# Reordering the last three heads of each attention round in a two-layer decode kernel

## The chip, the cores and the metric

The kernel runs on one core of a Trainium2 chip. The metric is device time in microseconds (us) of one launch; smaller is better. Everything is 32-bit floating point. The core's engines are TensorE (PE in the profile; its weight loads are PEld), VectorE (DVE), ScalarE (ACT), GpSimd (POOL, used only in the first microseconds) and SyncE (SP), which issues nearly all loads from device memory.

## The reference

A decode step for 4 sequences with one token each, model width 640. An attention layer and a dense layer, and then both again with the same weights:

```python
x = x + A(layernorm(x))     # 32 heads of 128, keys and values: the last 1024 of 4096 positions
x = x + B(layernorm(x))     # relu(x @ w1) @ w2, inner width 1728
x = x + A(layernorm(x))
x = x + B(layernorm(x))

# A, for each head h
q = x @ wq[:, h]                          # 4 x 128
p = softmax(q . k[b, h] * 128 ** -0.5)    # 4 x 1024, each sequence has its own cache
o = p . v[b, h]                           # 4 x 128
out += o @ wo[h]                          # back to 640
```

Each head needs its part of wq, its keys and values for four sequences, and its part of wo; one pass over all heads and both dense matrices is some 160 MB, read twice apart from what is kept on chip between the rounds.

## The kernel before, in words

**Records and buffers.** The host lays each head's data out as one record of 128 partitions by 9472 columns: wq (640 columns, from WQ), keys (4096, from K), values (4096, from V), wo (640, from WO). On chip there are five record buffers, `slot0` to `slot4`, used in turn, and a sixth, `ring`, which holds one more head of round 0 (head 26, SIXTH) and later the dense matrices w1 and w2 in pieces. The heads 27 to 31 stay in the five slots at the end of round 0 and are the first five of round 1, so they are not loaded again.

**Loads.** The list `items` holds all loads in an order written out by hand. `pump` issues from its head, on SP's queue, as long as the next piece's place on chip is free in the program's order; `done(key, lo, hi)` marks columns as used and pumps again. A load then waits on SP, at run time, for the instructions that last read its place. At most eight loads are under way, since a completion semaphore is used again only when its last load has landed. Most records are one load. The last three heads of a round, called a, b and c here, come in pieces in the order that `ending` gives. In round 0 the wo parts of the last five heads follow, and then w1 and w2, in eleven pieces, through three places of `ring`; each waits for the products on an earlier piece. In round 1 w1 goes into `ring` as a whole and w2 into a slot that came free.

**One head.** All engines run strictly in the program's order (`InOrder`). For a head:

- `query`: five products give q (128 x 4) in the first columns of a PSUM buffer `sc_ps[s]`, and DVE copies it to `qT`.
- `scores`: eight products give the scores of four sequences in the two banks of `sc_ps[s]`.
- `softmax`: DVE takes the maximum and scales it, ACT takes the exponential in place, with its sum in `tot[s]`.
- `weights`: DVE makes 1/sum (into `spread`, `rtot`, `mrt`), and for each half transposes the scores into `t_ps` and multiplies them into `wT`.
- `values`: four products for each half, with `wT` as the stationary operand, into `o_ps` (or, for the last head of a round, into the second bank of `sc_ps[0]`).
- `picks`: DVE picks the four wanted blocks out of that, in four operations, into `on`.
- `output_T`: a product with `pick` transposes it, DVE copies it to `oTs[:, i]`.
- `project`: four products with wo add it to the accumulator `acc`.

In the trace a 32-bit product stands as two passes, so `project` shows x8 and `query` x10.

**The loop of a round.** In steady state, while head n's values are taken, head n+1's scores and head n+2's query are interleaved: scores(n+1), softmax, values(n), picks, query(n+2), output_T, project, weights(n+1). Before the change it runs for all but two heads; the last two follow by hand, the second half of the weights of b behind the softmax of c. The outputs of the last `late` heads of a round (5 in round 0, where their wo comes last; 2 in round 1) are kept in `oTs`, and those in round 0 are projected at the end.

**Between attention and dense layer.** `center` sums `acc` over its columns, takes off the mean and prepares the squares; `mlp` takes the products with w1, in five blocks, with `deviation` (a product, DVE, a square root on ACT) behind the first, then relu on ACT, two transposes on DVE and the products with w2 in pieces. `busy(n)` is a product of n columns whose result nobody reads; it only keeps TensorE at work.

Of the kernel before, what the change touches and what calls it, by code (L numbers as in the profile page):

```python
# [32 lines left out]
F32 = mybir.dt.float32  # L33
AF = mybir.ActivationFunctionType
OP = mybir.AluOpType
# [3 lines left out]
P = 128  # L39
# [4 lines left out]
EPS = 1e-5  # L44
# [50 lines left out]
def decode_kernel(ctx: ExitStack, tc: tile.TileContext, xf, rec, w1, w2, out):  # L95
# [3 lines left out]
    ps = ctx.enter_context(tc.tile_pool(name="ps", bufs=1, space=PSUM))  # L99

    xT = sb.tile([P, FD], F32, name="xT")
    scratch = sb.tile([P, 480], F32, name="scratch")
    wT = scratch[:, :128].rearrange("p (i c j) -> p i c j", i=2, c=16)
    on = [scratch[:, 128:256], scratch[:, 288:416]]
    x_sb = scratch[:, :FD]
    same = scratch[:, FD:FD + P]
    blocks = xT.rearrange("p (k j) -> p k j", j=32)[:, :, :B]
    spread = scratch[:, 256:288]
    hT = scratch.rearrange("p (m j) -> p m j", j=32)
    oTs = sb.tile([P, LATE, B], F32, name="oTs")  # L110
    qT = sb.tile([P, B], F32, name="qT")
    of_batch = sb.tile([P, B], F32, name="of_batch")
    of_block = sb.tile([P, 4], F32, name="of_block")
    pick = sb.tile([P, B], F32, name="pick")
    mrt = sb.tile([P, B], F32, name="mrt")
    small = sb.tile([P, 14], F32, name="small")
    nmax, rtot, rstd, eps, eps_dh, ones, unused, sums, tot0, tot1 = (small[:, i:i + 1] for i in range(10))
    squares = small[:, 10:]
    tot = [tot0, tot1]
    slot = [sb.tile([P, REC], F32, name=f"slot{i}") for i in range(NS)]  # L120
    ring = sb.tile([P, RING], F32, name="ring")
# [23 lines left out]

    dve.tensor_reduce(of_block, same[:, :16].rearrange("p (c j) -> p c j", j=4), op=OP.add, axis=AX.X)
    dve.tensor_reduce(pick, same[:, :32].rearrange("p (c j) -> p j c", j=4), op=OP.add, axis=AX.X)
    dve.memset(small, EPS)
    dve.memset(eps_dh, EPS * DH)
    dve.memset(ones, 1.0)  # L150
    dve.memset(o_ps, 0.0)
# [24 lines left out]
    def ending(r, hs, late):  # L176
        a, b, c = hs[-3:]
        end = WO if late else REC
        for h, lo, hi in ((a, 0, V), (b, 0, V), (a, V, end), (c, 0, V), (b, V, end), (c, V, V + VH), (c, V + VH, end)):
            piece(r, h, lo, hi)  # L180
        if late:
            for h in hs[-1:] + hs[-LATE:-1]:
                piece(r, h, WO, REC)
# [116 lines left out]
    def xblock(k):  # L300
        return xT[:, 32 * k:32 * k + B]

    def query(r, h, s):
        q = sc_ps[s][:, :B]
        key = ("rec", r, h)
        for k in range(KB):
            pe.matmul(q, cols(key, WQ + k * DH, DH), xblock(k), start=(k == 0), stop=(k == KB - 1))
        done(key, WQ, K)
        dve.tensor_copy(qT, q)

    def scores(r, h, s, first=False):
        key = ("rec", r, h)
        for i in range(2):
            for b in range(B):
                pe.matmul(sc_ps[s][32 * b:32 * b + 4, 512 * i:512 * i + 512], qT[:, b:b + 1].to_broadcast([P, 4]),
                          cols(key, K + 512 * (B * i + b), 512), start=True, stop=True)
            done(key, K + VH * i, K + VH * i + VH)
            if first and i == 0:
                deviation(of_batch, eps_dh, float(DH))
                act.activation(unused, eps, AF.Exp)  # L320

    def softmax(s, first=False):

# [3 lines left out]
        dve.tensor_tensor(nmax, nmax, rstd, op=OP.mult)  # L327
        act.activation(sc_ps[s], sc_ps[s], AF.Exp, bias=nmax, scale=rstd, accum_out=tot[s])

    def weights(s, parts=(0, 1)):  # L330
        if 0 in parts:

            dve.transpose(spread, tot[s].to_broadcast([P, 32]))
            dve.reciprocal(rtot, spread[:, 0:1])
            dve.tensor_scalar(mrt, of_batch, rtot, None, op0=OP.mult)
        for i in parts:
            dve.transpose(t_ps, sc_ps[s][:, 512 * i:512 * i + 512])
            dve.tensor_tensor(wT[:, i], t_ps.rearrange("p (c j) -> p c j", j=32)[:, :, :B],
                              mrt.unsqueeze(1).to_broadcast([P, 16, B]), op=OP.mult)

    def values(r, h, last=False, fill=(0, 0)):
        key = ("rec", r, h)
        for i in range(2):
            for g in range(4):
                pe.matmul(outs[last][32 * g:32 * g + 16, :], wT[:, i, 4 * g:4 * g + 4, :].rearrange("p c j -> p (c j)"),
                          cols(key, V + VH * i + 512 * g, 512), start=(i == 0), stop=(i == 1))
            done(key, V + VH * i, V + VH * i + VH)
            for _ in range(fill[i]):
                busy(512, sc_ps[0])

    def picks(last):
        o, on_ = outs[last], on[last]
        dve.tensor_scalar(on_, o[:, :DH], of_block[:, 0:1], None, op0=OP.mult)
        for c in range(1, 4):
            dve.scalar_tensor_tensor(on_, o[:, DH * c:DH * c + DH], of_block[:, c:c + 1], on_, op0=OP.mult, op1=OP.add)

    def output_T(i, last=False):
        pe.matmul(outs[last][:, :B], on[last], pick, start=True, stop=True)
        dve.tensor_copy(oTs[:, i], outs[last][:, :B])

    def project(r, h, i, end):
        key = ("rec", r, h)
        for n in range(NB):
            pe.matmul(acc[32 * n:32 * n + B, :FD], oTs[:, i], cols(key, WO + n * FD, FD),
                      start=False, stop=end, skip_group_check=True)
        done(key, WO, REC)

    def mlp(r):


        h_ps, front, back = sc_ps[0][:, :512], t_ps[:, :224], sc_ps[0][:, 512:768]
        dve.memset(back[:, 208:240], 0.0)
# [16 lines left out]
        dve.transpose(scratch[:, 224:], back)  # L389
        key = ("w2", r)  # L390
        sizes = W2_SLOT if r else [size for name, size, _ in MLP_RING if name == "w2"]
        first = 0
        for i, size in enumerate(sizes):
            for s in range(first, first + size):
                m, n = TILES[s]
                w = cols(key, s * FD, FD)
                for part, q in ((m, n),) if m < 13 else ((13, n), (14, n + 2)):
                    pe.matmul(acc[32 * q:32 * q + B, :FD], hT[:, part, :B], w,
                              start=False, stop=(s >= len(TILES) - NB), skip_group_check=True)
            if r == 0 and i < len(sizes) - 2:  # L400
                busy(512)
            done(key, first * FD, (first + size) * FD)
            first += size
# [3 lines left out]
    pe.matmul(acc[:, :FD], ident, x_sb, start=True, stop=False, skip_group_check=True)  # L407
    for r in range(2):
        hs = order[r]
        late = LATE if r == 0 else 2  # L410
        center(r > 0)
        query(r, hs[0], 0)
        scores(r, hs[0], 0, True)
        softmax(0, True)
        query(r, hs[1], 1)
        weights(0)
        for n, h in enumerate(hs[:-2]):
            i = n - (H - late)
# [9 lines left out]
            weights(s, (0, 1) if n < H - 3 else (0,))  # L428
            if r == 0 and h == SIXTH:
                put_by()  # L430
            if r == 1 and hs[n + 2] == SIXTH:
                put_back()
        scores(r, hs[-1], 1)
        softmax(1)
        weights(0, (1,))
        values(r, hs[-2], 0, (0, 1))
        weights(1)
        picks(0)
        values(r, hs[-1], 1, (1, 0))
        picks(1)  # L440
        output_T(late - 2)
        for i in range(late - 3):
            project(r, hs[H - late + i], i, False)
        if late == 2:
            project(r, hs[-2], 0, False)
        output_T(late - 1, True)
        for i in (late - 3, late - 1, late - 2) if late > 2 else (1,):
            project(r, hs[H - late + i], i, i == late - 2 or late == 2)
        center(True)
        mlp(r)  # L450
    dve.tensor_copy(x_sb, acc[:, :FD])
# [39 lines left out]
```

## Time and profile before

| | |
|---|---|
| median of 3 runs | 719.93 us (717.66 to 720.21) |
| the profiled execution | 718.78 us, of which the span is 717.1 us |
| PE busy, share of the span | 516.8 us, 72% |
| DVE busy | 359.1 us, 50% |
| ACT busy | 93.0 us, 13% |
| read from memory | 301.56 MB, 421 GB/s over the span |
| mean granted TensorE clock | 0.797 of full speed |

Times in the rows are microseconds from the span's start. A timeline's row gives the start, the time taken, the engine, a line, the operation, out<-in with shapes, the number of instructions merged, and in brackets the idle time before and what ended it. A window's row gives the busy time of each engine (with the number of instructions that began), then the granted clock, the mean busy share of the 16 DMA engines, and GB/s. Nearly all instructions have line 87, the helper that keeps them in order, so groups are told apart by their tiles. Round 0's attention ends at about 367, its dense layer at about 391; round 1 follows to the end.

### The profile page before, as it was taken

How to read it: one execution, taken by the hardware profiler on the slowest of the kernel's cores; microseconds unless marked ns; L12 is line 12 of the kernel's file. 1: busy time of each engine (PE TensorE's matmuls, PEld its weight loads, DVE VectorE, ACT ScalarE, POOL GpSimd, SP SyncE). 2: the span in 40 equal slices, each digit the busy share in tenths (PEclk: the TensorE clock that was granted, in tenths of full speed). 3: DMA queues.
4: the chain of work that ended last, by engine and by line, in shares of the span. 5: the costliest groups of instructions: out<-in, count | busy, mean ns of one | idle time of the engine just before them, and what ended most of it. 6: DMA issues, size and time to landing. Idle time of an engine off the chain costs nothing.

```text
span 717.1 us, 8939 instructions
## 1 busy us (share of the span) xinstructions
PE 516.8 (72%) x3686; PEld 208.9 (29%) x3686; DVE 359.1 (50%) x1013; ACT 93.0 (13%) x145; POOL 1.1 (0%) x9
## 2 busy tenths in 40 slices
PE   4467756667686676857877998876857777666977
PEld 2132222313233232322223433332322322323323
DVE  3344545354455444545731677744545445444661
ACT  1201011010101101111200312201011010101111
POOL 0000000000000000000000000000000000000000
PEclk9977888687767777787899899977787578867797
DMA  9999999999999999999989999999999999999996
GB/s 377 435 435 434 435 428 430 436 434 433 430 430 434 435 432 435 431 427 424 424 345 333 409 434 428 444 425 434 436 433 436 422 431 436 438 434 418 429 426 286
DMA packets 15336, 302.21 MB, mean 421 GB/s; under 512 B 1712, under 2 KB 2240, under 8 KB 5312
## 3 DMA queue, kind: packets, MB, share of 16 engines
q1 hardware_dynamic: 15264, 301.64, 98.6%
q8 instruction: 29, 0.48, 0.2%
q14 instruction: 11, 0.09, 0.0%
q10 hardware_dynamic: 32, 0.01, 0.0%
HBM read 301.56 MB, written 0.08 MB: 421 GB/s over the span
## 4 chain that ended last, share of the span: by engine, by line
DMA 80%; PE 15%; DVE 3%; issue 1%; another core or an unknown queue 0%; DVEq 0%; SPq 0%
DMA slot<-rec 68%; PE sc_ps L87 8%; DMA ring<-rec 6%; PE o_ps L87 4%; DMA slot<-w 3%; PE acc L87 3%; DMA ring<-w 3%; DVE scratch L87 2%; DVE oTs L87 1%; DVE small L87 0%; DVE t_ps L87 0%; DVE ring L87 0%; DVE mrt L87 0%; DVE xT L87 0%
## 5 line engine op out<-in xcount | busy, mean ns | idle before, releaser
L87 PE MATMUL sc_ps<-xT,slot 128*128 128x4 f32 x620 | 99.5, 287 | 148.9 <-DMA slot<-rec 146.6
L87 PE MATMUL sc_ps<-slot,qT 128*4 128x512 f32 x992 | 197.1, 935 | 1.0 <-DVE qT L87 1.0
L87 PEld LDWEIGHTS sc_ps<-xT,slot 128*128 128x128 f32 x620 | 95.4, 238 | 203.7 <-issue 194.0
L87 ACT ACTIVATE sc_ps<-sc_ps,small 128x1024 f32<-128x1024 f32 (+1 forms) x68 | 76.6, 1127 | 551.4 <-DVE small L87 551.2
L87 PE MATMUL o_ps<-slot,scratch 128*16 128x512 f32 x960 | 132.9, 674 | 2.5 <-DVE scratch L87 1.6
L87 DVE TENSOR_REDUCE small<-sc_ps 128x1 f32<-128x1024 f32 x64 | 78.3, 1223 | 77.2 <-PE sc_ps L87 77.2
L87 DVE STREAM_TRANSPOSE t_ps<-sc_ps 128x512 f32<-128x512 f32 x128 | 93.2, 728 | 2.1
L87 DVE COPY qT<-sc_ps 128x4 f32<-128x4 f32 x64 | 10.2, 160 | 160.9 <-PE sc_ps L87 160.9
L87 PEld LDWEIGHTS o_ps<-slot,scratch 128*16 128x16 f32 x960 | 32.6, 118 | 127.4 <-issue 81.3
L87 DVE SCALAR_TENSOR_TENSOR scratch<-o_ps,of_block,scratch 128x128 f32<-128x128 f32 x186 | 65.2, 351 | 6.6
L87 PEld LDWEIGHTS sc_ps<-slot,qT 128*4 128x4 f32 x992 | 33.1, 115 | 83.1 <-issue 72.3
L87 PE MATMUL acc<-slot,oTs 128*4 128x160 f32 x496 | 36.9, 385 | 15.7 <-DVE oTs L87 15.7
L87 DVE TENSOR_SCALAR scratch<-o_ps,of_block 128x128 f32<-128x128 f32 x62 | 21.7, 350 | 32.1 <-PE o_ps L87 32.1
L87 PE MATMUL o_ps<-pick,scratch 128*128 128x4 f32 x124 | 28.4, 299 | 6.5 <-DVE scratch L87 6.5
L87 DVE TENSOR_TENSOR scratch<-t_ps,mrt 128x64 f32<-128x64 f32 x128 | 28.8, 225 | 4.7
L87 PEld LDWEIGHTS o_ps<-pick,scratch 128*128 128x128 f32 x124 | 25.2, 251 | 9.4 <-DVE scratch L87 8.5
L87 PE MATMUL sc_ps<-slot,small 128*1 128x512 f32 (+1 forms) x36 | 17.1, 568 | 0.0
L87 DVE COPY oTs<-o_ps 128x4 f32<-128x4 f32 x62 | 10.0, 162 | 14.0 <-PE o_ps L87 12.9
L87 DVE TENSOR_SCALAR mrt<-of_batch,small 128x4 f32<-128x4 f32 x64 | 14.7, 230 | 2.2
L87 DVE STREAM_TRANSPOSE scratch<-small 128x32 f32<-128x32 f32 x64 | 12.9, 202 | 1.6 <-ACT sc_ps L87 1.6
L87 PE MATMUL sc_ps<-ring,xT 128*4 128x432 f32 x80 | 10.0, 605 | 4.6 <-DMA ring<-w 3.0
L87 PEld LDWEIGHTS acc<-slot,oTs 128*4 128x4 f32 x496 | 7.0, 84 | 21.0 <-DVE oTs L87 20.9
(62 smaller groups left out, 116.3 us busy)
## 6 DMA issues: line engine op xcount, KB each, us to landing
slot<-rec SPq DMA_DIRECT2D x43, 4736.0 KB, 30.7
slot<-rec SPq DMA_DIRECT2D x17, 2368.0 KB, 19.8
slot<-rec SPq DMA_DIRECT2D x2, 4416.0 KB, 35.1
slot<-rec SPq DMA_DIRECT2D x7, 1024.0 KB, 7.7
ring<-w SPq DMA_DIRECT2D x8, 864.0 KB, 27.2
ring<-rec SPq DMA_DIRECT2D x1, 4576.0 KB, 41.9
slot<-rec SPq DMA_DIRECT2D x2, 2048.0 KB, 38.2
slot<-rec SPq DMA_DIRECT2D x3, 1344.0 KB
```

The costliest lines, as they stand in the source:

```text
L87: r = build(*args, **kwargs)
```

## The change

It has four parts.

1. In `ending`, the pieces a: wq and keys, b: wq and keys, a: values, c: wq and keys, ... become a, b and c: wq and keys, and then the values of a, b and c.
2. The work on a, b and c is written out anew. The loop ends one head earlier. Then: scores and softmax of b; the query product of c; weights of b into a second buffer `wTs[1]`, with the copy of c's query (`query_T`) behind their three small operations; scores and softmax of c; values of a, its picks and output; weights of c, into `wTs[0]`; values of b, its picks; values of c, with b's output between its halves; picks and output of c. Five `busy(512)` products (`warm`) stand between these, in place of the two that `fill` put there.
3. The memset on 32 columns of `sc_ps[0]`, needed by the dense layer, moves from the beginning of `mlp` to behind the last picks. The output of c is transposed into `o_ps`, not into `sc_ps[0]`.
4. In round 1 `late` becomes 3, and each output is projected as it comes. In round 0 the last head's output is projected first of the three that stand behind its copy.

To make room, four small tiles become columns of `small`, and `scratch` grows from 480 to 544 columns.

```diff
-    scratch = sb.tile([P, 480], F32, name="scratch")
-    wT = scratch[:, :128].rearrange("p (i c j) -> p i c j", i=2, c=16)
+    scratch = sb.tile([P, 544], F32, name="scratch")
+    wTs = [scratch[:, a:a + 128].rearrange("p (i c j) -> p i c j", i=2, c=16) for a in (0, 416)]
...
-        for h, lo, hi in ((a, 0, V), (b, 0, V), (a, V, end), (c, 0, V), (b, V, end), (c, V, V + VH), (c, V + VH, end)):
+        for h, lo, hi in ((a, 0, V), (b, 0, V), (c, 0, V), (a, V, end), (b, V, end), (c, V, V + VH), (c, V + VH, end)):
...
-    def query(r, h, s):
+    def query(r, h, s, copy=True):
...
-        dve.tensor_copy(qT, q)
+        if copy:
+            query_T(s)
+
+    def query_T(s):
+        dve.tensor_copy(qT, sc_ps[s][:, :B])
...
-    def weights(s, parts=(0, 1)):
...
+    def weights(s, w=0, between=None):
+        wT = wTs[w]
+        dve.transpose(spread, tot[s].to_broadcast([P, 32]))
+        dve.reciprocal(rtot, spread[:, 0:1])
+        dve.tensor_scalar(mrt, of_batch, rtot, None, op0=OP.mult)
+        if between:
+            between()
+        for i in range(2):
...
-    def values(r, h, last=False, fill=(0, 0)):
+    def values(r, h, last=False, w=0, between=None):
         key = ("rec", r, h)
+        wT = wTs[w]
         for i in range(2):
+            if i and between:
+                between()
...
-            for _ in range(fill[i]):
-                busy(512, sc_ps[0])
...
-        pe.matmul(outs[last][:, :B], on[last], pick, start=True, stop=True)
-        dve.tensor_copy(oTs[:, i], outs[last][:, :B])
+        pe.matmul(o_ps[:, :B], on[last], pick, start=True, stop=True)
+        dve.tensor_copy(oTs[:, i], o_ps[:, :B])
...
-        dve.memset(back[:, 208:240], 0.0)
...
-        late = LATE if r == 0 else 2
+        late = LATE if r == 0 else 3
...
-        for n, h in enumerate(hs[:-2]):
+        for n, h in enumerate(hs[:-3]):
...
-        scores(r, hs[-1], 1)
+        a, b, c = hs[-3:]
+
+        def warm(n):
+            for _ in range(n):
+                busy(512, sc_ps[0])
+
+        scores(r, b, 0)
+        softmax(0)
+        query(r, c, 1, False)
+        weights(0, 1, lambda: query_T(1))
+        scores(r, c, 1)
         softmax(1)
-        weights(0, (1,))
-        values(r, hs[-2], 0, (0, 1))
+        warm(1)
+        values(r, a)
+        picks(0)
+        warm(1)
+        output_T(late - 3)
         weights(1)
+        if r:
+            project(r, a, 0, False)
+        warm(1)
+        values(r, b, 0, 1)
         picks(0)
-        values(r, hs[-1], 1, (1, 0))
+        warm(1)
+        values(r, c, 1, 0, lambda: (output_T(late - 2), warm(1)))
+        if r:
+            project(r, b, 1, False)
+        else:
+            for i in range(late - 3):
+                project(r, hs[H - late + i], i, False)
         picks(1)
-        output_T(late - 2)
-        for i in range(late - 3):
-            project(r, hs[H - late + i], i, False)
-        if late == 2:
-            project(r, hs[-2], 0, False)
+        dve.memset(sc_ps[0][:, 720:752], 0.0)
         output_T(late - 1, True)
-        for i in (late - 3, late - 1, late - 2) if late > 2 else (1,):
-            project(r, hs[H - late + i], i, i == late - 2 or late == 2)
+        for i in (late - 1,) if r else (late - 1, late - 3, late - 2):
+            project(r, hs[H - late + i], i, i == (late - 1 if r else late - 2))
```

More of the change, by code (lines that the diff above doesn't have):

```diff
@@ L108, in decode_kernel @@
     spread = scratch[:, 256:288]
-    hT = scratch.rearrange("p (m j) -> p m j", j=32)
+    hT = scratch[:, :480].rearrange("p (m j) -> p m j", j=32)
     oTs = sb.tile([P, LATE, B], F32, name="oTs")
     qT = sb.tile([P, B], F32, name="qT")
[L112 to L118, printed above, removed]
+    small = sb.tile([P, 29], F32, name="small")
+    of_batch, of_block, pick, mrt = (small[:, 13 + B * i:13 + B * i + B] for i in range(4))
+    nmax, rtot, rstd, eps, eps_dh, ones, sums, tot0, tot1 = (small[:, i:i + 1] for i in range(9))
+    squares = small[:, 9:13]
     tot = [tot0, tot1]
@@ L147, in decode_kernel @@
     dve.tensor_reduce(pick, same[:, :32].rearrange("p (c j) -> p j c", j=4), op=OP.add, axis=AX.X)
-    dve.memset(small, EPS)
+    dve.memset(small[:, :13], EPS)
     dve.memset(eps_dh, EPS * DH)
@@ L319, in scores @@
                 deviation(of_batch, eps_dh, float(DH))
-                act.activation(unused, eps, AF.Exp)
+                act.activation(rtot, eps, AF.Exp)
     def softmax(s, first=False):
@@ L328, in softmax @@
         act.activation(sc_ps[s], sc_ps[s], AF.Exp, bias=nmax, scale=rstd, accum_out=tot[s])
-    def weights(s, parts=(0, 1)):
[L331 to L336, printed above, removed]
+    def weights(s, w=0, between=None):
[6 more added lines that the diff above has]
+        for i in range(2):
             dve.transpose(t_ps, sc_ps[s][:, 512 * i:512 * i + 512])
@@ L388, in mlp @@
         dve.transpose(scratch[:, :224], front)
-        dve.transpose(scratch[:, 224:], back)
+        dve.transpose(scratch[:, 224:480], back)
         key = ("w2", r)
@@ L427, in decode_kernel @@
                 project(r, h, 0, False)
-            weights(s, (0, 1) if n < H - 3 else (0,))
+            weights(s)
             if r == 0 and h == SIXTH:
```

## The prediction

> **What bounds the kernel now.** I read the page's header first, then the DMA columns of windows cut at the ends of the two rounds, then the timeline of each end.
>
> ```profile
> span 717.1 us, 8939 instructions
> ...
> DMA 80%; PE 15%; DVE 3%; issue 1%; another core or an unknown queue 0%; DVEq 0%; SPq 0%
> ```
>
> ```profile
> 340.00:366.00 26.00, 22.23 (x163) 6.96 (x163) 19.41 (x56) 3.88 (x6) 0.00 (x0) 0.87 1.00 422
> 366.00:396.00 30.00, 22.75 (x233) 8.03 (x232) 4.33 (x20) 3.14 (x7) 0.00 (x0) 0.99 0.90 321
> 396.00:454.00 58.00, 51.91 (x434) 22.90 (x434) 45.40 (x130) 12.95 (x20) 0.00 (x0) 0.88 1.01 428
> 454.00:708.00 254.00, 185.01 (x1263) 73.50 (x1256) 128.89 (x362) 31.37 (x48) 0.00 (x0) 0.76 1.00 431
> ```
>
> The last number of a window is GB/s. DMA carries the span, at 428 to 431 GB/s, except in 366 to 396 (round 0's MLP): 321 GB/s there is 30 x (1 - 321/430) = 7.6 us of transfers lost. Only two places can therefore move the time: how early that MLP begins, and how the last MLP ends. Everything between them is covered by a queue that is never empty.
>
> ```profile
> 369.65 5.98 DMA ring<-w
> 375.63 0.04 issue
> 375.68 0.95 PE sc_ps L87 x8
> 376.64 6.10 DMA ring<-w
> ```
>
> This is the chain of waits inside that MLP: a block of w1 or w2 is loaded when the PE has finished with an earlier one, and 6 us later its successor is used. So the MLP's start shifts the whole loop, and all that is loaded after it. What sets the start is round 0's last three heads, a, b and c (29, 30, 31):
>
> ```profile
> 346.02 1.90 PE L87 MATMUL sc_ps<-slot,qT 128*4 128x512 f32 x16
> ...
> 346.21 0.20 DVE L87 STREAM_TRANSPOSE scratch<-small 128x32 f32<-128x32 f32 x1
> ...
> 347.82 2.08 PE L87 MATMUL o_ps<-slot,scratch 128*16 128x512 f32 x16
> ...
> 348.71 1.22 DVE L87 TENSOR_REDUCE small<-sc_ps 128x1 f32<-128x1024 f32 x1
> ...
> 350.24 1.18 ACT L87 ACTIVATE sc_ps<-sc_ps,small 128x1024 f32<-128x1024 f32 x1 [4.59 <-DVE small L87]
> ...
> 351.53 1.25 PE L87 MATMUL sc_ps<-xT,slot 128*128 128x4 f32 x10 [1.63 <-ACT sc_ps L87]
> ...
> 353.03 2.39 PE L87 MATMUL sc_ps<-slot,qT 128*4 128x512 f32 x16
> ...
> 356.37 3.61 PE L87 MATMUL o_ps<-slot,scratch 128*16 128x512 f32 x16 [0.94 <-DMA slot<-rec]
> ...
> 357.01 1.18 ACT L87 ACTIVATE sc_ps<-sc_ps,small 128x1024 f32<-128x1024 f32 x1 [5.48 <-DVE small L87]
> ...
> 358.33 0.21 DVE L87 STREAM_TRANSPOSE scratch<-small 128x32 f32<-128x32 f32 x1 [0.54 <-ACT sc_ps L87]
> ...
> 358.78 0.23 DVE L87 TENSOR_SCALAR mrt<-of_batch,small 128x4 f32<-128x4 f32 x1
> ```
>
> In order: scores of b, weights of a, values of a, softmax of b (reduce, then ACT), query of c, scores of c, values of b, softmax and weights of c. The wait at 351.53 is, I take it, for c's K (ACT does not touch that bank for c yet), that at 356.37 for b's V. These two waits, 1.63 and 0.94 us, are all that DMA costs here. From there:
>
> ```profile
> 364.12 0.35 DVE L87 TENSOR_SCALAR scratch<-sc_ps,of_block 128x128 f32<-128x128 f32 x1 [1.64 <-PE sc_ps L87]
> ...
> 365.68 0.39 PE L87 MATMUL sc_ps<-pick,scratch 128*128 128x4 f32 x2 [0.68 <-DVE scratch L87]
> ...
> 366.00 1.05 PE L87 MATMUL acc<-slot,oTs 128*4 128x160 f32 x24
> 366.11 0.16 DVE L87 COPY oTs<-sc_ps 128x4 f32<-128x4 f32 x1 [0.41 <-PE sc_ps L87]
> ...
> 367.92 0.18 DVE L87 SCALAR_TENSOR_TENSOR xT<-o_ps,xT 128x20 f32<-128x20 f32 x1 [0.22 <-PE o_ps L87]
> ...
> 368.54 0.09 DVE L87 MEMSET sc_ps<- 128x32 f32 x1
> 368.68 0.91 PE L87 MATMUL sc_ps<-ring,xT 128*4 128x432 f32 x8 [0.80 <-DVE sc_ps L87]
> ...
> 370.56 1.02 PE L87 MATMUL sc_ps<-slot,small 128*1 128x512 f32 x2
> ...
> 371.32 0.19 PEld L87 LDWEIGHTS sc_ps<-ring,xT 128*4 128x4 f32 x8 [0.67 <-DMA ring<-w]
> ```
>
> Picks of c at 364.12, its output transposed, projected, centred, MLP at 368.68.
>
> **The change, part by part.**
>
> *Order of loads.* The four pieces aK, bK, aV, cK become aK, bK, cK, aV: same bytes, so a's V lands where c's K did (351.4) and c's K some 5 us earlier. SP's issues are only exchanged; the queue in front of them is not empty in either round (1.00 share above), so I cost the reordering on the queue at nothing; if that cover failed, it would cost at most the wait of an issue, about a microsecond. The waits at 351.53 and 356.37 go. What is late next is not DMA, but the chain PE-DVE, as follows.
>
> *Round 0, in the new order.* Up to the softmax of b nothing moves (350.24). Weights of b start 1.32 later (357.01 to 358.33): 351.56. The copy of c's query now stands behind three small DVE operations of these weights (0.45 + 0.23): 352.2, and 0.25 (352.78 to 353.03) on, scores of c start at 352.5. That is only 0.5 before today's 353.03, though c's K lies there 5 us earlier: DVE's order takes the place of the DMA wait. Then, at full clock:
> scores of c 1.90: 354.4; a warming product (two passes, 1.02 with its tail, 0.9 back to back): 355.3; values of a 2.08: 357.4. These were done at 347.82 before; now they stand behind the scores of c. Picks of a, 1.56 to the transposing product (364.12 to 365.68) and 0.1: 359.05; copy 0.43 later: 359.5. DVE then has the weights of c, 2.5 (346.21 to 348.71): 362.0. Beside it on the PE, warming 0.9 and values of b 2.08: 362.45. Picks of b: 364.1. On the PE meanwhile warming and the first half of c's values, 0.9 + 1.04: 364.4. Then in a row, since output_T(b) and a warming product stand between the halves: 0.4 + 0.9 + 1.04 = 366.75, picks of c at 366.8, against 364.12: **+2.7**. So the new order brings a's picks, one transposing product, and about 2.3 us of warming products onto the path; the second weight buffer (both weights ready early) saves nothing, as weights of c must wait for values of a anyway.
>
> Behind the picks: copy after 1.99 as before (364.12 to 366.11). Now all 24 passes of the projections follow it, where 8 preceded it (366.00): 8/24 of 1.05 = +0.35. The memset goes from the MLP's front to behind the picks, where DVE waits for the PE's 0.39 anyway. Before, the MLP waited for it (368.54 + 0.09, then 368.68), while xT was ready at 368.10: between 0.1 and 0.55, I take 0.45, since the PE's row names that very wait. Sum: 2.7 + 0.35 - 0.45 = **+2.6**.
>
> *The clock.* These are full-clock figures. The profile shows when it falls:
>
> ```profile
> 350.90:354.30 3.40, 2.74 (x24) 1.74 (x28) 1.96 (x8) 0.63 (x2) 0.00 (x0) 1.00 0.99 424
> 354.30:361.10 6.80, 5.86 (x32) 1.02 (x25) 5.04 (x14) 1.29 (x2) 0.00 (x0) 0.50 1.00 411
> ```
>
> The column before DMA's share is the granted clock: after a stretch with PE busy for 2.74 of 3.40 us, 1.25 of it a query of four moving columns, it was 0.50. In the new order the PE has only c's query between 347.9 and 352.5, so I expect a half-rate stretch at least as soon, on the scores of c, which then take some 1.4 us more (3.29 at half, below, against 1.90): +4.0. Of a late start, the 0.67 that the third block waits for its transfer at 371.32 is covered; I take 4.0 - 0.67 = **+3.3**. Bounds: +1.9 at full clock, +5.4 with two slow stretches and nothing covered.
>
> The Trainium skill, "TensorE: Matmul & The Clock Gate", Part 1, says the gate halves the clock after an idle window of about 3.4 us, and advises against longer idle gaps. By that rule no gap of the new order is long enough, the query standing in it, and the sum would be the full-clock one; the row of 350.90 to 354.30, with no such gap and the clock halved behind it, disagrees.
>
> *Round 1.* Same code, one more head with its projection:
>
> ```profile
> 683.24 1.18 ACT L87 ACTIVATE sc_ps<-sc_ps,small 128x1024 f32<-128x1024 f32 x1 [4.97 <-DVE small L87]
> ...
> 686.01 3.29 PE L87 MATMUL sc_ps<-slot,qT 128*4 128x512 f32 x16
> ...
> 696.76 0.35 DVE L87 TENSOR_SCALAR scratch<-sc_ps,of_block 128x128 f32<-128x128 f32 x1 [0.38 <-PE sc_ps L87]
> ...
> 700.21 0.32 DVE L87 TENSOR_REDUCE small<-acc 128x1 f32<-128x160 f32 x1 [0.84 <-PE acc L87]
> ...
> 702.29 1.62 PE L87 MATMUL sc_ps<-ring,xT 128*4 128x432 f32 x8 [0.80 <-DVE sc_ps L87]
> ...
> 709.18 1.90 PE L87 MATMUL acc<-slot,scratch 128*4 128x160 f32 x44
> ...
> 711.30 2.80 PE L87 MATMUL acc<-slot,scratch 128*4 128x160 f32 x68 [0.22 <-DMA slot<-w]
> ```
>
> Softmax of b at 683.24 as today; by the same steps scores of c at 685.5, values of a done 690.4, copy 692.5; project(a) 0.5, warming, values of b: 696.2; picks of b 697.8; then 698.15 + 0.4 + 0.9 + 1.04: picks of c at 700.55, against 696.76: +3.8. The projection of b no longer stands behind the picks: 1.99 + 0.2 + 0.7 + 0.1 = 3.0 to the centring, where it was 3.45 (696.76 to 700.21): -0.45; the memset -0.45: +2.9. A slow stretch on the scores of c: +1.4. Today's end has little slack: w2 products are 1.90 + 2.80 = 4.7 of the 4.92 between 709.18 and 714.10, idle 0.22. So an earlier MLP can gain 0.2 at most, a later one counts nearly in full. If the MLP itself ran at full clock (its first block 0.91 as at 368.68, not 1.62), 0.7 comes back. I take 2.9 + 1.4 - 0.2 - 0.7 = **+3.4**; bounds +2.0 (full clock throughout) and +5.5 (two slow stretches, nothing back).
>
> *Names folded into `small`, `unused` replaced by `rtot`, query_T split off:* same instructions, no added wait on the path; nothing, or 0.2 either way where a copy is queued one place later.
>
> **Sum.** 718.78 (the profiled execution: span 717.1 and 1.7 around it) + 3.3 + 3.4 = **725.5**. The median of the runs, 719.93, is 1.15 above that execution; I leave the sum on the execution. Bounds: 718.78 + 1.9 + 2.0 = 722.7 and 718.78 + 5.4 + 5.5 = 729.7.
>
> **Rivals.**
> *Full clock in both ends.* The warming products (five against two) could keep the PE warm. For it: the clock was 0.99 in 366 to 396, where such products are issued. Against: the first one stands behind the scores of c, after the quiet stretch. Time: 722.7, 0.4% above the median.
> *Only one end counts.* The loop of round 0's MLP may take up the delay: the six microseconds from issue to use could shrink when fewer transfers stand in front. For it: 5.98 us is long for 864 KB at 430 GB/s (2.0 us). Against: the DMA is drained by then. Time: 718.78 + 3.4 = 722.2; if the last end is milder too, down to 720.
> *Faster: the values follow V at once.* If DVE gets through weights and picks of a and b before c's V lands, then c's second half of values follows that landing. The loads of V are behind all K, some 8 us behind today's values of a, and b's V lands at 356.3; c's V 4.9 us later at 2048 KB and 430 GB/s, by 361.2, would give picks at 362.4, 1.7 earlier; with memset and projection 1.8, and in round 1 at most 0.2: 718.78 - 2.0 = 716.8; with c's V in somewhat sooner down to 715.3, past the bound of 0.5%. It decides if picks of b are over by 361; my count has 364.1.
>
> **How the numbers follow.** A measurement of this kernel tells about 0.5% (3.6 us) from no change. Forecast (both ends longer, 723.5 and up): 0.58. Full clock: 0.20. One end: 0.14. Faster rival: 0.08, of which 0.06 beyond 0.5%. So slower 0.58, same 0.36 (both middle cases and the rest), faster 0.06. Range: from 718.5 (the middle cases with their milder ends) to 730.0 (upper bound); the forecast's own is 722.7 to 729.7.
>
> **What the next profile would show.** Right: no DMA wait before c's query or b's values; values of a behind the scores of c; picks of c in round 0 near 368 rather than 364.12, first w1 products near 372 instead of 368.68, GB/s in that MLP below 321 over a longer stretch; round 1's w2 products without a wait for DMA, starting later than 709.18 and last. The MLP's first product should follow xT, not the memset. Wrong: scores of c clearly before 352, DVE idle between softmax of c and picks of a for less than I count, or warming products that hide behind DVE; above all if MLP starts before 368.7 in round 0.

## The result, and the profile after

The changed kernel takes 724.16 us (median of six runs, 721.49 to 724.47); the kernel before took 718.93 beside it (717.62 to 720.21). The ratio is 1.0064, interval 1.0041 to 1.0087. The forecast was 725.5 and "slower", so the total is 1.3 us off. But two errors of opposite sign stand behind that: one term of the sum was not there, and one cost was left out. Here and below, "lost" means microseconds of DMA time: the length of a window, times the difference in GB/s between the two kernels, over 430.

The header of the page of the changed kernel, and its chain that ended last; below them, windows (last number GB/s, before it DMA share and granted clock):

```profile
span 722.5 us, 8956 instructions
...
DMA 78%; PE 17%; DVE 4%; issue 1%; ACT 0%; ACTq 0%; DVEq 0%; SPq 0%
```

```profile
0.00:60.00 60.00, 31.41 (x178) 13.47 (x178) 23.10 (x65) 8.24 (x12) 1.14 (x9) 0.91 0.98 416
60.00:290.00 230.00, 163.19 (x1068) 67.34 (x1072) 110.43 (x308) 25.92 (x40) 0.00 (x0) 0.74 1.00 431
290.00:340.00 50.00, 37.46 (x246) 15.00 (x238) 25.81 (x69) 6.45 (x10) 0.00 (x0) 0.74 1.00 428
340.00:366.00 26.00, 21.85 (x139) 6.69 (x138) 18.45 (x54) 3.91 (x7) 0.00 (x0) 0.87 1.00 416
...
366.00:454.00 88.00, 75.45 (x641) 30.19 (x644) 45.80 (x140) 14.80 (x24) 0.00 (x0) 0.88 0.94 376
...
454.00:708.00 254.00, 185.74 (x1286) 74.83 (x1282) 134.25 (x375) 31.10 (x48) 0.00 (x0) 0.78 1.00 430
```

The same windows of the kernel before, as far as the prediction does not show them:

```profile
0.00:60.00 60.00, 32.90 (x178) 14.22 (x178) 23.05 (x65) 8.24 (x12) 1.12 (x9) 0.89 0.98 417
60.00:290.00 230.00, 160.52 (x1064) 66.62 (x1068) 110.14 (x307) 25.90 (x40) 0.00 (x0) 0.75 1.00 433
290.00:340.00 50.00, 35.62 (x252) 13.26 (x244) 26.71 (x73) 6.47 (x10) 0.00 (x0) 0.80 0.99 427
...
366.00:454.00 88.00, 74.66 (x663) 30.93 (x666) 49.73 (x150) 16.09 (x26) 0.00 (x0) 0.92 0.97 392
```

The profiled execution of the changed kernel took 724.17 us, 5.39 more than that of before. Lost, window by window: 0.1 up to 60, 1.1 in 60 to 290, -0.1 up to 340, 0.4 up to 366, 3.3 in 366 to 454, 0.6 after that: 5.3 in all. So the account closes with transfers alone, as far as whole GB/s can tell (one of them is about 0.5 us in either of the two long windows). Two things in it were not foreseen. About 1.7 us are lost at 431 against 433 GB/s and 430 against 431, in stretches whose code the change does not touch, apart from round 1's tail at the end of the second. And nothing is left for round 1's end. Two rows of each kernel's end show the latter: the timeline of the changed kernel is

```profile
707.68 0.91 PE L87 MATMUL sc_ps<-ring,xT 128*4 128x432 f32 x8 [0.27 <-DVE xT L87]
...
708.84 3.08 PE L87 MATMUL sc_ps<-ring,xT 128*4 128x432 f32 x32
...
712.93 1.89 PE L87 MATMUL acc<-slot,scratch 128*4 128x160 f32 x44
716.67 2.82 PE L87 MATMUL acc<-slot,scratch 128*4 128x160 f32 x68 [1.85 <-DMA slot<-w]
```

The last products start at 716.67, where they started at 711.30: 5.37 later, which is the whole difference, and what they wait for is w2's load, 1.85 us. The products of w1 had time to spare.

Round 0's end, from the timeline of the changed kernel:

```profile
346.67 3.50 PE L87 MATMUL sc_ps<-slot,qT 128*4 128x512 f32 x16
...
350.10 1.33 PE L87 MATMUL sc_ps<-xT,slot 128*128 128x4 f32 x10
...
351.75 1.18 ACT L87 ACTIVATE sc_ps<-sc_ps,small 128x1024 f32<-128x1024 f32 x1 [5.46 <-DVE small L87]
...
353.87 3.46 PE L87 MATMUL sc_ps<-slot,qT 128*4 128x512 f32 x16 [2.44 <-DVE qT L87]
...
357.60 2.29 PE L87 MATMUL o_ps<-slot,scratch 128*16 128x512 f32 x13
...
364.69 0.35 DVE L87 TENSOR_SCALAR scratch<-o_ps,small 128x128 f32<-128x128 f32 x1
...
368.53 0.35 DVE L87 TENSOR_SCALAR scratch<-sc_ps,small 128x128 f32<-128x128 f32 x1 [1.70 <-PE sc_ps L87]
...
370.12 0.09 DVE L87 MEMSET sc_ps<- 128x32 f32 x1
...
370.73 1.00 PE L87 MATMUL acc<-slot,oTs 128*4 128x160 f32 x24 [0.25 <-DVE oTs L87]
...
372.83 0.91 PE L87 MATMUL sc_ps<-ring,xT 128*4 128x432 f32 x8 [0.27 <-DVE xT L87]
```

The first row is b's scores, ahead of everything that the new order moves: they began 0.65 later than before and ran at half rate (3.50 instead of 1.90 us), so the softmax of b stands at 351.75, 1.5 later than the 350.24 of before. From there the prediction can be followed step by step: c's query has no DMA wait, its scores wait 2.44 us for DVE's copy and run at half rate (3.46), the values of a come behind them, the picks of c stand at 368.53 (before 364.12), the MLP starts at 372.83 (before 368.68) and follows xT, not the memset.

### The profile page after: what moved, and what is told of

It is laid out like the page before. It is cut to its first block, busy times and chain, and to the rows that moved or that the text cites. A ratio compares the mean times of both kernels' runs of the same rounds, so it can differ in the third digit from the quotient of the medians.

```text
span 722.5 us, 8956 instructions
## 1 busy us (share of the span) xinstructions
PE 524.7 (73%) x3698; PEld 212.2 (29%) x3698; DVE 359.6 (50%) x1013; ACT 93.1 (13%) x145; POOL 1.1 (0%) x9
## 4 chain that ended last, share of the span: by engine, by line
DMA 78%; PE 17%; DVE 4%; issue 1%; ACT 0%; ACTq 0%; DVEq 0%; SPq 0%
DMA slot<-rec 73%; PE sc_ps L87 10%; PE o_ps L87 4%; DMA slot<-w 3%; PE acc L87 3%; DVE scratch L87 2%; DMA ring<-w 2%; DVE small L87 1%; DVE oTs L87 1%; DVE t_ps L87 0%; ACT sc_ps L87 0%; DVE ring L87 0%; DVE qT L87 0%; DVE xT L87 0%; ACTq L87 0%
## 5 line engine op out<-in xcount | busy, mean ns | idle before, releaser
L87 PE MATMUL sc_ps<-slot,qT 128*4 128x512 f32 x992 | 202.4, 957 | 6.0 <-DVE qT L87 6.0
L87 DVE SCALAR_TENSOR_TENSOR scratch<-o_ps,small,scratch 128x128 f32<-128x128 f32 x186 | 65.2, 351 | 6.6
L87 DVE TENSOR_SCALAR scratch<-o_ps,small 128x128 f32<-128x128 f32 x62 | 21.7, 350 | 34.9 <-PE o_ps L87 34.9
L87 PE MATMUL o_ps<-small,scratch 128*128 128x4 f32 x128 | 29.6, 302 | 10.1 <-DVE scratch L87 10.1
L87 DVE TENSOR_TENSOR scratch<-t_ps,small 128x64 f32<-128x64 f32 x128 | 28.8, 225 | 4.4
L87 PEld LDWEIGHTS o_ps<-small,scratch 128*128 128x128 f32 x128 | 26.3, 254 | 15.6 <-DVE scratch L87 15.5
L87 PE MATMUL sc_ps<-slot,small 128*1 128x512 f32 (+1 forms) x48 | 22.0, 548 | 0.0
L87 DVE TENSOR_SCALAR small<-small 128x4 f32<-128x4 f32 x64 | 14.8, 231 | 2.2
L87 ACT ACTIVATION_READ_ACCUMULATOR sc_ps<-sc_ps,small 128x1 f32 x64 | 12.2, 191 | 0.0
```

The source lines that it names most:

```text
L87: r = build(*args, **kwargs)
```

## Experiments

All kernels compute the whole result. Ratios are to the kernel before, run on the same chip; 0.1% is 0.72 us.

**One round at a time.** `e1_round0_only` and `e2_round1_only` have the new code in one round and the old one in the other, with the changed kernel's tiles.

```diff
+NEW = (True, False)
...
-        for n, h in enumerate(hs[:-3]):
+        for n, h in enumerate(hs[:-3] if NEW[r] else hs[:-2]):
...
+        if not NEW[r]:
+            scores(r, hs[-1], 1)
+            softmax(1)
+            weights(0, parts=(1,))
...
```

(`NEW` is (False, True) in the second; behind `if not NEW[r]` stand the lines of the kernel before.)

> The new order of loads, tail and memset in round 0 only; round 1 ends as before. Theory A (only round 0's end counts, since the loads of round 1 end later than its products): nearly the whole loss stays, 722.5 to 724.5 us against 718.9 before. Theory B (both ends count, as predicted): round 0's share of 3.3 us alone, less than half of it measured after the rest is taken off, about 721 to 722. Theory C (something that differs from the first microsecond on, such as the layout on chip, slows the transfers): a shift of 1 us or more at the 29th load, as in the changed kernel.

> The new order of loads, tail and memset in round 1 only; round 0 ends as before. Theory A: within 0.5 us of before, 718.4 to 719.5, with the products on w2 waiting for the last transfers. Theory B: 3.4 us slower, about 722. Theory C: about 1 us slower, with the shift present at the 29th load.

Measured: 1.0067 (1.0046 to 1.0088) for round 0 alone, 1.0051 (1.0034 to 1.0068) for round 1 alone. Each half costs about what the whole does, 1.0064. Costs of two places that simply add would have given 1.0118. So either the two hide one another, or all three kernels share something that is neither. What they share are the sizes of the tiles, and with them the places of the buffers.

**Where the buffers lie.** In the kernel before, `slot0` begins at byte 3072 of a partition, behind the small tiles. The changed kernel's small tiles take 192 bytes more, so `slot0` begins at 3264, and all five slots and `ring` move up with it. A slot is 37888 bytes, 148 times 256, so every buffer starts at a multiple of 256 before, and 192 beyond one after. `e9_shift_192` is the kernel before, with a tile of 48 columns that nothing uses:

```diff
+    pad = sb.tile([P, 48], F32, name="pad")
```

> The kernel before with nothing changed but an unused tile of 192 bytes a partition ahead of the five record buffers, so that they begin at byte 3264 of a partition, as in the changed kernel, and not at 3072 (a multiple of 512). Theory C (the place of the buffers slows every load): 721.5 to 723 us against 719.2, and the 29th load lands about 1 us later than in the kernel before. If the layout does not matter: within 0.4 us of before.

Measured: 1.0059 (1.0034 to 1.0084). An unused tile costs about as much as the whole change. Its windows:

```profile
60.00:290.00 230.00, 162.98 (x1064) 66.95 (x1068) 110.16 (x306) 25.89 (x40) 0.00 (x0) 0.73 1.00 431
...
366.00:454.00 88.00, 73.54 (x674) 29.73 (x678) 50.57 (x152) 16.09 (x26) 0.00 (x0) 0.96 0.98 396
454.00:708.00 254.00, 181.26 (x1246) 72.78 (x1242) 127.77 (x360) 31.36 (x48) 0.00 (x0) 0.76 1.00 429
```

431 and 429 GB/s in the steady stretches, as in the changed kernel or below, and no loss in the stretch of round 0's end. The reverse edit is `e10_after_aligned`: the changed kernel with its small tiles behind `ring` and a short pad, so that `slot0` is at 3072 again.

```diff
-    oTs = sb.tile([P, LATE, B], F32, name="oTs")
-    qT = sb.tile([P, B], F32, name="qT")
+    pad = sb.tile([P, 16], F32, name="pad")
+    slot = [sb.tile([P, REC], F32, name=f"slot{i}") for i in range(NS)]
+    ring = sb.tile([P, RING], F32, name="ring")
+    oTs = sb.tile([P, LATE + 1, B], F32, name="oTs")
+    qT = oTs[:, LATE]
...
-    slot = [sb.tile([P, REC], F32, name=f"slot{i}") for i in range(NS)]
-    ring = sb.tile([P, RING], F32, name="ring")
```

> The changed kernel with its small tiles moved behind the ring, so that the record buffers begin at byte 3072 again; no other change. Theory C: 2 to 3.5 us faster than the changed kernel, 720.5 to 722, the rest being round 0's later MLP. If the layout does not matter: 723.5 to 724.5 as before.

Measured: 1.0028 (1.0012 to 1.0044), less than half of the changed kernel's 0.64%. Its windows and its end of round 0 (`qT` is a column of `oTs` here):

```profile
60.00:290.00 230.00, 161.92 (x1072) 66.17 (x1076) 111.33 (x309) 25.89 (x40) 0.00 (x0) 0.75 1.00 433
...
366.00:454.00 88.00, 74.60 (x635) 29.89 (x637) 46.97 (x141) 14.79 (x24) 0.00 (x0) 0.88 0.96 377
454.00:708.00 254.00, 186.93 (x1288) 75.19 (x1284) 133.11 (x374) 31.46 (x49) 0.00 (x0) 0.77 1.00 432
```

```profile
350.86 3.59 PE L87 MATMUL sc_ps<-slot,oTs 128*4 128x512 f32 x16 [1.47 <-DVE oTs L87]
...
370.52 0.91 PE L87 MATMUL sc_ps<-ring,xT 128*4 128x432 f32 x8 [0.27 <-DVE xT L87]
```

The steady stretches are back at 433 and 432; the loss of 366 to 454 stays (377 against 392, 3.1 us). So the two costs are separate, and windows away from the edited code tell them apart.

Does it take 3072, or any multiple of 256? `e14_base_2816` is the kernel before with its small tiles behind `ring`, so that `slot0` is at 2816 = 11 x 256, not a multiple of 512:

```diff
+    pad = sb.tile([P, 16], F32, name="pad")
+    slot = [sb.tile([P, REC], F32, name=f"slot{i}") for i in range(NS)]
+    ring = sb.tile([P, RING], F32, name="ring")
...
-    slot = [sb.tile([P, REC], F32, name=f"slot{i}") for i in range(NS)]
-    ring = sb.tile([P, RING], F32, name="ring")
```

> The kernel before with its small tiles behind the ring, so that the record buffers begin at byte 2816, a multiple of 256 but not of 512. If what counts is 256 bytes (the Trainium skill, DMA: Bandwidth & Descriptors, How a descriptor splits into AXI transactions: a descriptor that does not start at a multiple of 256 bytes costs part of a transaction more), within 0.4 us of before. If 512 counts: as slow as the shift of 192, 722 to 724. If it is not the buffers but the tiles' own place: also unlike before.

Measured: 0.9998 (0.9978 to 1.0017), with

```profile
60.00:290.00 230.00, 162.56 (x1068) 66.79 (x1072) 110.59 (x308) 25.91 (x40) 0.00 (x0) 0.74 1.01 434
```

A multiple of 256 is enough, and moving the tiles costs nothing in itself. Places beyond a multiple by other than 192 bytes were not tried.

The traces also hold the time of every single transfer, which is sharper than whole GB/s. A full row of a record, 37888 bytes, stands there as one transfer, 5504 times in each trace. Its mean time is 1403.2 to 1403.3 ns in each of the eight kernels whose buffers begin at a multiple of 256, and 1407.5 to 1407.6 ns in each of the six at 3264, whatever their order of work: 0.31% more. Of the 707 us for which loads keep the DMA engines busy in the kernel before, that is 2.2 us, an estimate of what the place of the buffers costs.

**Round 1 alone, aligned.** `e12_round1_aligned` is `e2_round1_only` with the tile order of `e10_after_aligned`.

> The new order, tail and memset in round 1 only, buffers at 3072. Theory A with C (round 1's end is covered by the loads, the 3.3 us of the run with this tail in round 1 came from the layout): within 0.5 us of before, 718.7 to 719.8. Theory B (round 1's end costs about 3.4 by itself): 722 or more.

Measured: 1.0001 (0.9983 to 1.0019). The new end of round 1 costs nothing that can be measured. Its timeline (its helper's line is L88):

```profile
674.73 1.90 PE L88 MATMUL sc_ps<-slot,oTs 128*4 128x512 f32 x16
...
695.85 0.35 DVE L88 TENSOR_SCALAR scratch<-sc_ps,small 128x128 f32<-128x128 f32 x1 [1.70 <-PE acc L88]
...
699.62 0.91 PE L88 MATMUL sc_ps<-ring,xT 128*4 128x432 f32 x8 [0.27 <-DVE xT L88]
...
707.30 2.71 PE L88 MATMUL acc<-slot,scratch 128*4 128x160 f32 x44 [2.08 <-DMA slot<-w]
711.00 4.49 PE L88 MATMUL acc<-slot,scratch 128*4 128x160 f32 x68 [0.99 <-DMA slot<-w]
```

The MLP starts 2.7 us earlier than before (702.29), gains nothing by it, and waits for both pieces of w2; the last lands at 711.00, where the kernel before started at 711.30. Here the tail had begun 4.9 us earlier than before (softmax of b at 678.34 against 683.24), so this run alone does not try a late MLP. The changed kernel does, and so does `e10_after_aligned`: their MLPs start 5.4 and 3.6 later than before, and their last products wait for w2 all the same, 1.85 us in the rows above and 1.09 here:

```profile
705.92 0.91 PE L87 MATMUL sc_ps<-ring,xT 128*4 128x432 f32 x8 [0.27 <-DVE xT L87]
...
714.14 2.79 PE L87 MATMUL acc<-slot,scratch 128*4 128x160 f32 x68 [1.09 <-DMA slot<-w]
```

The window of 366 to 454 of `e12_round1_aligned` has 392 GB/s, as before:

```profile
366.00:454.00 88.00, 76.20 (x644) 30.07 (x644) 47.74 (x142) 15.29 (x25) 0.00 (x0) 0.88 0.98 392
```

**Parts of the new end.** `e4_old_order` is the changed kernel with the old order of loads, `e3_no_warm` the changed kernel without its five products.

```diff
-        for h, lo, hi in ((a, 0, V), (b, 0, V), (c, 0, V), (a, V, end), (b, V, end), (c, V, V + VH), (c, V + VH, end)):
+        for h, lo, hi in ((a, 0, V), (b, 0, V), (a, V, end), (c, 0, V), (b, V, end), (c, V, V + VH), (c, V + VH, end)):
```

> The changed kernel's tail with the loads in the order of before (a's values ahead of c's keys). If VectorE's order sets when c's scores begin, as the sum had it, c's keys landing 5 us later move c's scores by less than 0.5 us, and the time stays within 0.7 us of the changed kernel, 723.5 to 724.8. The rival, that the early keys do help the new tail: 726 or more.

Measured: 1.0126 (1.0107 to 1.0146), nearly twice the changed kernel's loss; I had expected less than 0.7 us of difference. The timeline tells why:

```profile
353.15 2.27 PE L87 MATMUL sc_ps<-xT,slot 128*128 128x4 f32 x10 [4.02 <-DMA slot<-rec]
...
355.67 3.59 PE L87 MATMUL sc_ps<-slot,qT 128*4 128x512 f32 x16 [0.26 <-DVE qT L87]
...
375.95 0.91 PE L87 MATMUL sc_ps<-ring,xT 128*4 128x432 f32 x8 [0.27 <-DVE xT L87]
```

The new tail asks for c's keys ahead of the values of a, so a load that stands behind a's values blocks the PE for 4.02 us, and the query and the scores behind it are at half rate. The MLP starts 3.1 us later than in the changed kernel (372.83). The new order of loads does its part: it is the new order of work that costs.

```diff
         def warm(n):
-            for _ in range(n):
-                busy(512, sc_ps[0])
+            return
```

> The changed kernel without its five warming products in each round's tail. If they lie on the path, as the sum had it (about 2.3 us at full clock), and the clock does not fall further, round 0's MLP starts about 2 us earlier than in the changed kernel and the time is 722 to 722.5. If the clock falls without them, the products at half rate take that back: no change, 724, or slower.

Measured: 1.0080 (1.0054 to 1.0106): no gain, the second of the two cases that I had named. The interval overlaps that of the changed kernel, so the times alone do not tell the two apart. The MLP starts no earlier, and at half rate:

```profile
361.83 3.53 PE L87 MATMUL o_ps<-slot,scratch 128*16 128x512 f32 x16 [0.25 <-DVE oTs L87]
...
372.80 1.62 PE L87 MATMUL sc_ps<-ring,xT 128*4 128x432 f32 x8 [0.27 <-DVE xT L87]
```

The values of b take 3.53 us instead of about 2.4 (362.19 to 364.6 in the changed kernel, a warming product between), the first block of w1 1.62 instead of 0.91: the warming products pay for themselves, though they stand on the path.

**Towards a better version.** `e16_aligned_warm_gap` is `e10_after_aligned` with filling products where the PE waits for the copy of c's query.

```diff
         query(r, c, 1, False)
+        for _ in range(3):
+            busy(512, o_ps)
```

> The changed kernel, buffers at 3072, with three unread products between c's query and c's scores, where the PE waits for the weights of b. If the half-rate stretch there is what adds 1.4 us or more to round 0's tail, the scores of c take 1.9 to 2.4 us instead of 3.5 and the time is 1 to 2 us below the same kernel without them, 719.5 to 720.7. If not: 721.5 as there.

Measured: 1.0014 (0.9997 to 1.0031).

```profile
349.30 2.73 PE L87 MATMUL o_ps<-slot,small 128*1 128x512 f32 x6
351.84 1.91 PE L87 MATMUL sc_ps<-slot,oTs 128*4 128x512 f32 x16
...
369.26 0.91 PE L87 MATMUL sc_ps<-ring,xT 128*4 128x432 f32 x8 [0.27 <-DVE xT L87]
```

```profile
366.00:454.00 88.00, 74.29 (x650) 29.79 (x650) 48.69 (x146) 16.09 (x26) 0.00 (x0) 0.92 0.97 390
```

The scores of c take 1.91 instead of 3.59 us, the MLP starts 1.26 earlier, and 390 GB/s is nearly the 392 of before. The intervals of the two kernels overlap, so the trace shows this gain and the times do not separate it. In round 1, w2's products show no wait for their load here:

```profile
710.09 4.33 PE L87 MATMUL acc<-slot,scratch 128*4 128x160 f32 x112
```

So the cover of round 1's end is thin: with the loads this early, the engines' chain and the load end about together.

`e11_interleave_aligned` puts the values of a ahead of the weights of b and picks b behind them, so that c's softmax has cover. `e15_interleave_2` is the same with the projections moved behind the values of c and three filling products ahead of the values of a.

```diff
+        values(r, a)
         weights(0, 1, lambda: query_T(1))
         scores(r, c, 1)
+        picks(0)
+        values(r, b, 1, 1)
         softmax(1)
-        warm(1)
-        values(r, a)
-        picks(0)
-        warm(1)
         output_T(late - 3)
...
-        warm(1)
-        values(r, b, 0, 1)
...
```

> Buffers at 3072, the new order of loads, and another order of work in the tail: values of a ahead of the weights of b, picks of a behind those weights, values of b in the bank that b's scores leave, picks of b while ACT takes the exponential of c, and one warming product instead of five. Counted from rows of the kernel before: picks of c in round 0 at about 362.7 against 364.12, the MLP about 2 us earlier than there. Theory A with C: 716.5 to 718.5 us, at or below before. If the clock falls throughout the tail: equal to before.

> The interleaved tail again, buffers at 3072, with the projections behind the values of c (in the first try they waited 1.5 us for wo, ahead of those values) and three unread products ahead of the values of a. Picks of c in round 0 at 363 to 364, MLP start 1 to 3.5 us earlier than in the first try: 717.5 to 720 us. If the clock stays low: 721 and more.

Measured: 1.0078 (1.0051 to 1.0105) and 1.0014 (0.9994 to 1.0033). The first, 724.62 us, missed its forecast by some 6 us; the second, 719.87, is within its own. In the first, the values of a waited 3.07 us for their load and then ran at half rate, and the projections stood ahead of the values of c and waited 1.52 for wo, which is loaded behind all values:

```profile
351.36 3.61 PE L87 MATMUL o_ps<-slot,scratch 128*16 128x512 f32 x16 [3.07 <-DMA slot<-rec]
...
362.62 2.32 PE L87 MATMUL acc<-slot,oTs 128*4 128x160 f32 x24 [1.52 <-DMA slot<-rec]
```

`e6_memset_warm` goes the other way: the kernel before, with the memset behind the last picks and two filling products ahead of c's query.

```diff
-        dve.memset(back[:, 208:240], 0.0)
...
+            if n == H - 3:
+                busy(512, sc_ps[n % 2])
+                busy(512, sc_ps[n % 2])
...
+        dve.memset(sc_ps[0][:, 720:752], 0.0)
```

> The kernel before, its own layout and order of loads, with two edits: the memset behind the last picks, and two unread products where the PE waits for c's keys. The memset alone should start round 0's MLP 0.4 us earlier; if the products keep the clock up for the values of b, 1 to 1.5 us more: 717 to 718 us where before has 718.9. If the clock falls anyway: within 0.5 us of before.

Measured: 0.9993 (0.9976 to 1.0010). The MLP of round 0 starts 1.1 us earlier than before, at 367.58, and follows xT; the 717 to 718 us that I had hoped for did not come (median 719.02), and in the time nothing can be told. No version was measurably faster than the kernel before.

## Why the prediction came out as it did

**Right: the mechanism of round 0's end. Its size came out partly by luck.** The step "picks of c at 366.8" at full clock and 1.4 more for the slow scores gives 368.2; the changed kernel had 368.53. But 1.5 us of that stand ahead of the new order, where the prediction had "nothing moves": the softmax of b came at 351.75, not 350.24, behind b's slow scores. From ACT's exponential of b to the picks of c it took 13.9 us before, 16.8 in the changed kernel and 17.5 in the aligned one (348.74 to 366.22); predicted were 16.6 at full clock and 18.0 with a slow stretch. With the clock kept up, in `e16_aligned_warm_gap`, it took 15.2 (349.72 to 364.96). So the count at full clock was 1.3 too long, and the slow stretch cost some 2.2 and not 1.4; the two errors nearly cancel. (The values of a that "were done at 347.82 before" began there and ended at 349.90; no sum uses this.) The term was +3.3. The windows of 366 to 454 show 3.3 and 3.1 lost; the times of `e10_after_aligned` give 2.0 (0.9 to 3.2), in which round 1's end is contained. This window differs by 2.5 us between kernels that all have the old end of round 0 (384 GB/s in `e2_round1_only`, 396 in `e9_shift_192`), so the agreement is no better than a microsecond or two. The GB/s in 366 to 396 went from 321 to 311, as foreseen.

**Right: the clock.** It fell behind the quiet stretch with only c's query in it, as the row of 350.90 to 354.30 of the kernel before had suggested. The changed kernel's windows show the stretch and the one behind it:

```profile
350.24:353.65 3.41, 1.19 (x10) 1.10 (x10) 1.86 (x5) 1.30 (x2) 0.00 (x0) 1.00 0.99 420
...
353.65:357.06 3.41, 3.19 (x16) 0.53 (x17) 1.99 (x6) 0.00 (x0) 0.00 (x0) 0.50 0.99 416
```

The Trainium skill, "TensorE: Matmul & The Clock Gate", Part 1, puts the drop down to an idle window of about 3.4 us. The PE was busy 1.19 us of this stretch and the clock halved all the same, so the rule, read as "no work at all", is too mild here; its length agrees, as each of these two windows of 3.41 us holds a single clock. `e16_aligned_warm_gap`, which fills the gap, kept the clock at 1.00. Which share of such a window has to be busy, the runs do not show.

**Right: the memset** left the path (0.27 behind xT instead of 0.80 behind the memset), and its 0.45 is too small to be seen in the time.

**Wrong: round 1's term, +3.4; measured 0** (`e12_round1_aligned`, -1.2 to +1.4). The failing steps are "softmax of b at 683.24 as today", the size of the tail behind it, and "a later one counts nearly in full". The tail has no fixed start: the softmax of b stood at 678.34 in `e12_round1_aligned`, at 684.90 in `e10_after_aligned` and at 686.83 in the changed kernel, where b's scores ran at half rate (3.29 us from 681.93, against 1.90 from 679.63 before). From there to the MLP's first product it took 19.05 us before, and 21.28, 21.02 and 20.85 in these three: about 2 longer, where 2.9 + 1.4 = 4.3 had been counted. Of a late MLP more comes back than the 0.7 that I gave: from its first product to w2's it took 6.9 us before (702.29 to 709.18) and 5.25 in the changed kernel (707.68 to 712.93), with the clock full. So on the engines' chain itself some 0.2 of the 3.4 is left in the changed kernel (1.8 longer, 1.6 back), and the end is set by w2's last load. I had also foreseen w2's products "without a wait for DMA"; they waited 1.85.

**Wrong: "nothing, or 0.2 either way" for the names and tile sizes.** I looked only for instructions in this part of the change. There are none; the 64 columns more in `scratch`, with the other sizes, moved every load's target. With that the premise "only two places can therefore move the time" fell: the rate of the loads moves it everywhere. The cost of the shift is 4.2 us by the times of `e9_shift_192` (2.4 to 6.0), 3.7 by those of `e2_round1_only` (2.4 to 4.9), whose new end of round 1 costs nothing by `e12_round1_aligned`, 2.2 by the times of the single rows, and 1.7 by the windows of the changed kernel. The profiled execution of `e9_shift_192`, 720.49 us, was one of the fastest of its nine (720.16 to 725.32) and itself only 1.7 above that of before. The rows are the sharpest of these figures; whether the times of the runs hold something beyond them is open. The halves, 0.59% and 0.28%, add to more than the 0.64% measured, though within the intervals. That the cost is there, and is the layout, rests on three things: padding alone brings it, alignment alone takes it away, and the GB/s of 60 to 290 and the time of a single row go with it in all fourteen kernels.

So 718.78 + 3.3 + 3.4 came near the 724.16 because the layout stood in for round 1, which is luck. The rival "only one end counts" was right that one does, but had the wrong one: it let round 0's loop take up its delay and kept round 1's 3.4. Its 722.2 is near the 721.72 of `e10_after_aligned`, the changed kernel without the shift, only because the two terms were of one size.

**Early keys** I had costed at nothing, since DVE takes the place of the DMA wait. `e4_old_order` shows that the new order of work needs them: with the old order of loads, its MLP starts 3.1 us later than in the changed kernel.

## What to carry to other kernels

When a change alters the size of any tile, list where the large buffers begin before and after, even if no instruction differs. Here buffers at multiples of 256 bytes (3072 and 2816) were filled faster than those 192 bytes beyond one, so begin there a buffer that a stream of loads fills. Before explaining a difference by the edited code, compare GB/s in a steady stretch that the edit does not touch, and check that the losses of all windows add up to the difference. A delay in a tail counts only against what that tail waits for last: where the final load sets the end, the engines' chain can be some microseconds later or earlier for nothing.

## What the hardware showed that I had not expected

Loads into buffers 192 bytes beyond a multiple of 256 ran at 431 GB/s, into aligned ones at 433 to 434, in the same 230 us of the same work; a row of 37888 bytes took 1407.6 instead of 1403.2 ns, 0.31% more. The Trainium skill, "DMA: Bandwidth & Descriptors", section "How a descriptor splits into AXI transactions", says that a transaction starts at a multiple of 256 bytes, and that a descriptor which does not start there pays for the unused beats of its first transaction. By that page a row of a record (37888 bytes) takes 1184 beats of 32 bytes aligned, and 8 + 147 x 8 + 6 = 1190 at 192 beyond: an estimate of 0.5%, if it holds for the place that a load writes, and a row is one descriptor. The measured 0.31% of a row is of this order, though smaller; that 2816 costs nothing agrees with the page in the condition. The runs do not show the beats themselves.
